# Loads of v tied to a mask of the slot, and one weight load moved behind a later product, in a threshold attention with SwiGLU

## The chip, the core and the metric

One core of a Trainium2 chip runs the whole program. The metric is the device time of one execution in microseconds, the median of several runs. The engines are named as in the profile: PE (TensorE, with PEld for its weight loads), DVE (VectorE), ACT (ScalarE), POOL (GpSimd) and SP (SyncE, which here only issues DMAs). All work of an engine runs in the order in which the program lists it, and an instruction whose semaphores are not yet reached holds up everything behind it on that engine.

## The reference

```python
batch, n_heads, seq, head_dim = (8, 8, 576, 64)
n_tokens, d_model, d_ff = (4608, 512, 1536)

scores = scale * np.matmul(q, k.transpose(0, 1, 3, 2))
thresh = np.max(scores, axis=-1, keepdims=True) - tau
scores = np.where(scores >= thresh, scores, -1000000000.0)
scores = scores - np.max(scores, axis=-1, keepdims=True)
attn = np.exp(scores)
attn = attn / (np.sum(attn, axis=-1, keepdims=True) + 1e-09)
attn_out = np.matmul(attn, v)
x = attn_out.transpose(0, 2, 1, 3).reshape(B * S, H * D)
g = x @ w_gate
silu = g * (1.0 / (1.0 + np.exp(-g)))
out = (silu * (x @ w_val)) @ w_out
```

q, k and v are 32-bit floats; the weights arrive as 64-bit floats.

## The kernel before

The attention of batch b+1 runs beside the feed-forward of batch b. After a first stretch (about 130 us) in which the first batch's attention is begun and the weights are turned into 32-bit numbers, the main loop runs over 28 pairs of heads, `halved`, with three slots each (`x` = 0, 1, 2), so twelve slots (`kk` = 0 to 11) make up a block `b` of one batch. In a slot TensorE computes scores of a third of the queries (`slot_scores`, L1865), VectorE finds the row maxima (L1886, L1888), ScalarE takes exponentials (L1911), VectorE masks them against the threshold and sums them (`masks`, L1913, six to a slot, one for each head and query group), ScalarE or POOL divides by the sums, and VectorE turns the result (L1941).

The product with v of a pair, `attend` (L1946, its matmuls on L1962), is issued in slot `x` = 1 of the next pair, just ahead of that slot's scores. It reads `vall`, which has one place for a pair's v. `prepare_v` therefore loads the v of the current pair after this product, by four DMAs of 144 KB (`load_v`, L441) on SP's queue. That v is read by the `attend` of the following pair.

Between the scores TensorE runs the feed-forward: gates and values in groups (`Group`, products on L1052, seven products `p1`, `p5`, `p2`, `p6`, `p3`, `p7`, `p4` for a group), and output products (`Outputs` on L1331 in the first blocks, `Deep` with its nested products on L1598 in the later ones). From the third batch on (`DEEP`) the weights of a group and sums of them are streamed from memory into `flow`, which has room for two groups. `load_flow` (L982, its DMA on L985) loads a group in two parts: part 0 is 1024 KB (the first four operands), part 1 is 768 KB (the last three, read by the group's `p3`, `p7` and `p4`). Inside `Deep` the same room holds intermediate sums, so `next_flow` (L1838) asks for the next block's groups 0 and 1 as the output products free it.

`Deep.steps` is `p1, gates_end, p2, p7, p6, p4, p5, p3`. `CD` says how many of these steps are done in which slot: the last two, `p5` and `p3`, fall in slots `kk` = 0 and 1 of the next block. Right behind `p3` the gates of the next block begin.

The order of the instructions on VectorE, ScalarE, POOL and SP is made by `Plan`: each piece of work is a `job` with an engine, an assumed duration, the jobs it depends on and a rank, and the planner lists them by the times it computes. TensorE's order is as written. A job's dependencies decide only the order. What an instruction waits for on the chip follows from the data: a DMA into `vall` waits for the matmuls that still read it, and for an earlier write to the same place.

```python
        if x == 1 and n > 0:
            prepare_v(seg, attend(halved[n - 1]))
```

Of the kernel before, what the change touches and what calls it, by code (L numbers as in the profile page):

```python
# [27 lines left out]
class Plan:  # L28
# [12 lines left out]
    def job(self, eng, took, fn, *deps, rank=1, lag=0.0, moves=0.0):  # L41
        j = Job(eng, took, fn, rank, lag, moves)
        for d in deps:
            if isinstance(d, Job) and d.end is None:
                d.then.append(j)
                j.waits += 1
            elif d is not None:
                j.ready = max(j.ready, self.after(d, eng) if isinstance(d, Job) else d + self.HOP)
        if not j.waits:
            self.open[eng].append(j)  # L50
        return j
# [45 lines left out]
    def pe(self, took, fn, *deps):  # L97
        self.force(*deps)
        for d in deps:
            if d is not None:  # L100
                self.t = max(self.t, (d.end if isinstance(d, Job) else d) + self.HOP)
        self.run(self.t)
        fn()
        self.t += took
        return self.t + self.PIPE
# [39 lines left out]
def kernel(  # L145
# [11 lines left out]
    nc = tc.nc  # L157
# [51 lines left out]
    vall = const.tile([P, 2 * NJ * D], F32, name="vall")  # L209
# [627 lines left out]
    job, pe = plan.job, plan.pe  # L837
# [42 lines left out]
    def take(name, full=False):  # L880
        free = [b for b in banks if (not b.held if b.fixed is not None else b.n in turns)]
        if full:
            free = [b for b in free if b.full]
            return Hold(min(free, key=Bank.free_at), name) if free else None
        n = sum(b.full for b in free)
        return Hold(min(free, key=lambda b: (b.full and n == 1, max(b.free_at(), plan.t))), name)
# [17 lines left out]
    def pool_tt(out, a, b, op):  # L904
        return lambda: nc.gpsimd.tensor_tensor(out=out, in0=a, in1=b, op=op)  # L905
# [84 lines left out]
    def x_place(c, kh):  # L990
        lo = c % 2 * XW if kh == 0 else 2 * XW
        return xall[:, lo:lo + XW].rearrange("p (t c n) -> p t c n", t=2, c=2)
# [42 lines left out]
    class Group:  # L1035
# [32 lines left out]
        def p5(self):  # L1068
            self.take_b()
            self.e = take("pe")  # L1070
            m = self.mul(self.e, self.w[2], xs[0], True, *self.w_deps[2], *ready_x[self.c][1], *self.e.deps)
            self.e.bank.full = True
            s, old = turn_of(s_bufs)
            self.s = s
            self.s5 = job("ACT", 0.55, lambda: nc.scalar.activation(s.ap, self.e.rows(), AF.Copy, scale=0.5), m, *old, rank=0)
# [38 lines left out]
        def p3(self):  # L1114
            m = self.mul(self.e, self.w[5], xs[2], False, self.s5, *self.w_deps[5], *ready_x[self.c][4])
            u = self.u1_buf
            g1 = job("DVE", 0.7, lambda: nc.vector.scalar_tensor_tensor(out=u.ap, in0=self.e.rows(), scalar=0.5, in1=u.ap, op0=ALU.mult,
                                                                        op1=ALU.add), m, self.u1, rank=0)
            self.e.read_by(g1)
            self.e.done(True)  # L1120
            self.finish(0, u, g1, self.a, self.m2)
# [405 lines left out]
    class Deep:  # L1527
# [250 lines left out]

        def p5(self):
            m = self.nested(4, self.x, False, *self.c6)  # L1780
            self.next_flow(1, 1, m)
            t, t7 = self.spaces[0:2]
            self.c5 = self.copies(t, self.x, m, *self.z)
            n, j = self.combine(t7, job("POOL", 2.2, pool_tt(t7, t7, t, ALU.add), *self.c5, *self.c7, rank=1))
            self.ship(1, 1, n, j)
            for b in u_list:
                b.jobs = [*b.jobs, j]

        def p3(self):
            m = self.nested(2, self.x, False, *self.c5)  # L1790
            n, j = self.combine(self.x, m, psum=True)
            self.done(self.x, j)
            self.ship(0, 1, n, j)
# [52 lines left out]
    sc_users = []  # L1846
# [99 lines left out]
    def attend(seg):  # L1946
        i = seg["i"]
        b, cc = divmod(i, NP)
        base = seg["p"]
        p = pall[:, base:base + 2 * NK * SH].rearrange("p (k h j q) -> p h k j q", h=2, j=NK, q=G)  # L1950
        vr = seg["v"]
        R, rows = 2, P // 2
        holds = [take("xa") for _ in range(R)]
        assert cc < 2 or "last_product" not in state

        def fn():
            for j in range(NK):
                for a in range(R):
                    rs = slice(a * rows, (a + 1) * rows)
                    for x in range(NG):  # L1960
                        h, ds = x // 2, slice(x % 2 * G, (x % 2 + 1) * G)
                        nc.tensor.matmul(holds[a].ap()[x * G:(x + 1) * G, 0:SH].rearrange("d (i q) -> d i q", q=G),  # L1962
                                         vr[rs, h, j, ds], p[rs, h, :, j, :], start=(j == 0), stop=(j == NK - 1))

        m = pe(4.5, fn, *seg["turned"], seg["vj"], *holds[0].deps, *holds[1].deps)
        kh, c2 = divmod(cc, 2)
        xk = x_place(b, kh)[:, :, c2, :].rearrange("p t (i a q) -> p a t i q", a=2, q=G)
        xl = xlast[:, cc, :].rearrange("p (a q) -> p a q", a=2)
        js = x_jobs.setdefault(b, [])
        lo, at_last = 0, 2 * NT * G  # L1970
        for a in range(R):
            def copy(a=a):
                nc.scalar.copy(xk[:, a], holds[a].ap()[:, lo:lo + 2 * NT * G].rearrange("p (t i q) -> p t i q", t=2, q=G))
                nc.scalar.copy(xl[:, a], holds[a].ap()[:, at_last:at_last + G])
            js.append(job("ACT", 0.65, copy, m, last_store[0] if cc == 0 else None,
                           *(sixth_kept if b == DEEP + 1 else ()), rank=0))
            holds[a].read_by(js[-1])
            holds[a].done(False)
            holds[a].bank.full = False
        if cc == NP - 1:  # L1980
            store_last(b, *js)
        if cc >= 2:
            token_sums(b, c2, js[2 * c2:2 * c2 + 2] + js[2 * cc:] + [stores[2]], "DVE" if tail[0] else "POOL")
        return m

    def store_last(b, *deps):
        w = S - SM
        last_store[0] = job("SP", 0.1, lambda: nc.sync.dma_start(out=last_hbm[:, :, b * w:(b + 1) * w], in_=xlast), *deps, lag=3.0)
# [24 lines left out]
    def prepare_v(seg, *deps):  # L2013
        seg["vj"] = job("SP", 1.7, lambda: load_v(seg), *deps, lag=2.3, moves=2.6)

    halved = segs[2 * NP:]
# [107 lines left out]
    for s, (n, x) in enumerate((n, x) for n in range(len(halved)) for x in range(NU3)):  # L2124
        seg = halved[n]
        i, t = seg["i"], seg["tiles"][x]
        b, kk = s // NS + 1, s % NS
        if x == 1 and n > 0:
            prepare_v(seg, attend(halved[n - 1]))
        pss, mark = slot_scores(seg, t)  # L2130
        if s == 0:
            next(last, None)
            attend_tile()
            next(last, None)
            flip()
            plan.t += 2.4
            plan.free.update(DVE=2.0, ACT=2.5)
        elif s == 1:
            box = []
            m = pe(1.0, lambda: attend_tile(lambda *y: box.extend(y)))  # L2140
            j = job("ACT", 0.27, box[1], m, rank=0)
            banks[taken[id(box[0])][0]].jobs.append(j)
            give_back(box[0])
            next(last, None)
            store_last(0, j)
        if s == 1:
            prepare_v(seg)
        at_, pooled, max_by_act = (kk, POOLED, MAX_BY_ACT) if b > DEEP else (s, FIRST_POOLED, FIRST_MAX_BY_ACT)
        slot_rest(seg, t, pss, mark, pooled.get(at_, 0), at_ in max_by_act, 1 if x == NU3 - 1 else 2)
        if x == 0 and n + 1 < len(halved):  # L2150
            prepare_next(i + 1, plan.t)
        if s == 0:
            joins = rest_of_weights()
        block_part(b, kk)
        if 2 <= s < 6:
            output_sums(s - 2, plan.t, *joins)
        if s in WS:
            g, place = WS[s]
            weight_sums(g, place, plan.t, *joins, stores.get({2: 0, 3: 1, 4: 3, 5: 4}.get(g)))
        if 10 <= s < 10 + NF2:  # L2160
            g = s - 10
            weight_part(g, summed_g[g], plan.t)
        if s > NS and x and (g := (s - NS) * (NU3 - 1) // NU3) < NF2:
            store_plain(g, parts[g], plan.t)
# [71 lines left out]
```

## Time and profile before

| | us |
|---|---|
| median of 3 runs | 1360.17 (1358.74 to 1366.19) |
| profiled execution | 1362.1 |
| its span, first to last instruction | 1360.2 |
| granted TensorE clock, mean | 0.999 |
| an attention product (L1962), 144 records | 4.39 |
| scores of a slot (L1865), 64 records | 1.63 |
| eight records of a gate product (L1052, 128x256) | 1.73 |
| 768 KB weight load `big<-sums_hbm`, issue to landing, median | 4.4 |
| 1024 KB weight load, issue to landing, median | 5.3 |
| 144 KB load of v, issue to landing, median | 2.9 |

A "record" is one line of the trace; each 32-bit matmul of the program leaves two of TensorE's matmuls and two weight loads. The profile has a page with shares by engine, by slice of the span and by chain, and the trace behind it can be asked for the waits of one engine, for instructions in order of time, and for busy time in given stretches. In a timeline each row has the start, the time it took, the engine, the source line, the operation, what was written from what, and a count; a bracket has the engine's idle time ahead of it and what ended it. "Issue" there means that nothing which the profile shows was waited for. For a DMA issue on SP's queue (SPq) the time is that of issuing; the transfer follows.

TensorE's rows overlap by some 0.1 us where one matmul starts before the last one's modelled end.

### The profile page before, as it was taken

The numbers are of one execution on the slowest core, as the hardware profiler recorded it, in microseconds if no ns is written. First come the engines' busy times: TensorE is split into PE (matmuls) and PEld (weight loads), VectorE is DVE, ScalarE is ACT, GpSimd is POOL, SyncE is SP. The second block draws the span as 40 slices with busy tenths as digits, with TensorE's granted clock in tenths as the row PEclk, the third lists the DMA queues.
The fourth block names the chain that finished last, engine by engine and source line by source line (L and its number), as shares of the span: only waits on it lengthen the run. The fifth ranks groups of instructions, "written<-read, shape, count | busy, mean of one in ns | idle before, by whom it ended". The sixth has DMA issues, their size and how long they took to land.

```text
span 1360.2 us, 39655 instructions
## 1 busy us (share of the span) xinstructions
PE 1341.3 (99%) x15770; PEld 1115.8 (82%) x15770; DVE 1072.6 (79%) x2839; ACT 876.0 (64%) x2260; POOL 689.1 (51%) x717
## 2 busy tenths in 40 slices
PE   8999999999999999999999999999999999999998
PEld 6777777787788788878887888878887789999998
DVE  6888898878887777778787877877787776787786
ACT  6888777777756767677776766776767774330330
POOL 2588397543464669624982379426952495000000
PEclk9999999999999999999999999999999999999999
DMA  8752424555525532554164515553255405424411
GB/s 196 183 187 93 81 56 134 149 137 145 152 68 162 148 98 68 152 159 127 37 188 129 150 36 147 137 151 87 89 156 145 114 22 174 158 78 147 157 61 32
DMA packets 210760, 166.28 MB, mean 122 GB/s; under 512 B 166288, under 2 KB 182160, under 8 KB 205200
## 3 DMA queue, kind: packets, MB, share of 16 engines
q1 hardware_dynamic: 206656, 162.83, 42.2%
q8 instruction: 125, 2.05, 0.6%
q10 hardware_dynamic: 3920, 0.92, 0.4%
q14 instruction: 59, 0.48, 0.1%
HBM read 141.30 MB, written 22.41 MB: 120 GB/s over the span
## 4 chain that ended last, share of the span: by engine, by line
PE 94%; DVE 2%; POOL 1%; DMA 1%; issue 1%; ACT 0%; DVEq 0%; SPq 0%; POOLq 0%
PE pb L1052 18%; PE pa L1052 12%; PE px L1598 12%; PE sc L1865 10%; PE xa L1962 9%; PE pe L1052 9%; PE po L1331 5%; PE py L1598 3%; PE pv L1256 2%; PE pg L1256 2%; PE sc L1213 2%; PE py L1607 2%; PE sc L468 1%; PE pe L1213 1%; PE tp L538 1%; PE xa L569 1%
## 5 line engine op out<-in xcount | busy, mean ns | idle before, releaser
L1913 DVE SCALAR_TENSOR_TENSOR pall<-sc,th,pall 128x288 f32<-128x288 f32 x504 | 244.4, 513 | 58.4 <-ACT pall L1911 39.9
L1052 PE MATMUL pb<-xall,big 128*128 128x256 f32 x1152 | 273.3, 380 | 0.0
L1911 ACT ACTIVATE pall<-sc,nm 128x288 f32<-128x288 f32 x504 | 232.8, 497 | 39.0 <-DVE pall L1913 38.9
L1052 PEld LDWEIGHTS pb<-xall,big 128*128 128x128 f32 x1152 | 216.5, 190 | 30.7 <-issue 2.2
L1941 DVE STREAM_TRANSPOSE pall<-pall 128x576 f32<-128x576 f32 x252 | 188.9, 764 | 30.7 <-ACT pall L1939 22.3
L1939 ACT ACTIVATE pall<-pall,ri 128x288 f32<-128x288 f32 x413 | 189.9, 528 | 30.8 <-DVE ri L1927 30.4
L1052 PE MATMUL pa<-xall,big 128*128 128x256 f32 x768 | 183.6, 382 | 0.0
L905 POOL TENSOR_TENSOR hall<-hall,tmp 128x512 f32<-128x512 f32 x80 | 102.5, 1282 | 155.3 <-DVE hall L1105 137.1
L1886 DVE TENSOR_REDUCE mx<-sc 128x2 f32<-128x576 f32 x168 | 125.7, 748 | 52.4 <-PE sc L1865 52.2
L1052 PEld LDWEIGHTS pa<-xall,big 128*128 128x128 f32 x768 | 142.9, 190 | 22.4 <-issue 2.7
L1865 PE MATMUL sc<-kT,qT 64*32 64x288 f32 (+1 forms) x5376 | 147.1, 345 | 5.0 <-issue 3.4
L1865 PEld LDWEIGHTS sc<-kT,qT 64*32 64x32 f32 x5376 | 95.9, 106 | 57.1 <-issue 18.4
L1052 PE MATMUL pe<-xall,big 128*128 128x256 f32 x576 | 137.3, 381 | 0.0
L1962 PE MATMUL xa<-pall,vall 64*32 64x288 f32 x4032 | 129.3, 404 | 0.6 <-issue 0.6
L1052 PEld LDWEIGHTS pe<-xall,big 128*128 128x128 f32 x576 | 108.4, 190 | 17.0 <-issue 2.5
L1962 PEld LDWEIGHTS xa<-pall,vall 64*32 64x32 f32 x4032 | 74.0, 107 | 48.2 <-issue 6.8
L1936 POOL TENSOR_SCALAR pall<-pall,ri 128x288 f32<-128x288 f32 x91 | 45.2, 511 | 93.3 <-DVE ri L1927 92.9
L1921 ACT COPY sums<-sums 32x6 f32<-32x6 f32 x336 | 66.6, 198 | 36.8 <-DVE pall L1913 31.9
L905 POOL TENSOR_TENSOR tmp<-tmp 128x512 f32<-128x512 f32 (+1 forms) x41 | 56.5, 1377 | 63.7 <-ACT tmp L1127 62.2
L905 POOL TENSOR_TENSOR big<-hall 128x384 f32<-128x384 f32 (+2 forms) x69 | 65.3, 970 | 33.2 <-PE pa L1052 26.1
L1104 ACT ACTIVATE vall<-tmp 128x512 f32<-128x512 f32 x96 | 60.1, 629 | 27.8 <-POOL tmp L905 13.5
L1888 DVE TENSOR_REDUCE mx<-sc 128x1 f32<-128x288 f32 x168 | 75.0, 447 | 0.0
(279 smaller groups left out, 2503.2 us busy)
## 6 DMA issues: line engine op xcount, KB each, us to landing
big<-sums_hbm SPq DMA_DIRECT2D x42, 1024.0 KB, 5.3
big<-sums_hbm SPq DMA_DIRECT2D x48, 768.0 KB, 4.4
vall<-in_v_dram SPq DMA_DIRECT2D x112, 144.0 KB, 2.9
out_dram<-big SPq DMA_DIRECT2D x32, 256.0 KB, 2.4
qT<-in_q_dram SPq DMA_DIRECT2D x112, 72.0 KB, 4.8
kT<-in_k_dram SPq DMA_DIRECT2D x112, 72.0 KB, 2.9
wo<-in_moe_w_gate_dram SPq DMA_DIRECT2D x16, 384.0 KB, 3.5
wo<-in_moe_w_val_dram SPq DMA_DIRECT2D x16, 384.0 KB, 4.1
```

Source lines behind the costliest of these rows:

```text
L905: return lambda: nc.gpsimd.tensor_tensor(out=out, in0=a, in1=b, op=op)
L1052: nc.tensor.matmul(ps[:, i], w[:, k_, i * P:(i + 1) * P], x[:, k_, :], start=first and i == k_ == 0, stop=True, skip_group_check=True)
L1331: nc.tensor.matmul(ps, h(f), w[:, f, :], start=(f == 0), stop=(f == NF2 - 1))
L1598: nc.tensor.matmul(ps, a[:, f, :], ws[n][:, f, :], start=bank_ not in begun, stop=True, skip_group_check=True)
L1865: nc.tensor.matmul(pss[h][(slice(g * G, (g + 1) * G), *part)], qT[hs, col:col + G], kT[hs, c * SH + keys[0]:c * SH + keys[1]], start=True, ...
L1886: rs.append(job("DVE", 0.72, lambda n=n, tile_=tile_: nc.vector.tensor_reduce(out=mx[:, n:n + 2, 0], in_=tile_[:, :, 0:SH], axis=AX.X, op= ...
L1888: rs.append(job("DVE", 0.42, lambda n=n, tile_=tile_: nc.vector.tensor_reduce(out=mx[:, n + 2:n + 3, 0], in_=tile_[:, :, SH:SH + SQ], axis ...
L1911: ej = job("ACT", 0.42, lambda x=x, n=n: nc.scalar.activation(ps[x], scs[x], AF.Exp, bias=nm[:, n:n + 1]), ej, masks.get((h, u - 1)), rank=0)
L1913: masks[x] = job("DVE", 0.45, lambda x=x, n=n: nc.vector.scalar_tensor_tensor(out=ps[x], in0=scs[x], scalar=th[:, n:n + 1], in1=ps[x], op0 ...
L1939: scaled.append(job("ACT", 0.46, lambda x=x, n=n: nc.scalar.activation(x, x, AF.Copy, scale=ri[:, n:n + 1]), rj, rank=rank))
L1941: seg["turned"].append(job("DVE", 0.72, lambda both=both: nc.vector.transpose(out=both, in_=both), *scaled, rank=rank))
L1962: nc.tensor.matmul(holds[a].ap()[x * G:(x + 1) * G, 0:SH].rearrange("d (i q) -> d i q", q=G), vr[rs, h, j, ds], p[rs, h, :, j, :], start=( ...
```

## The change

```diff
--- before.py
+++ after.py
@@ -1778,7 +1778,6 @@
 
         def p5(self):
             m = self.nested(4, self.x, False, *self.c6)
-            self.next_flow(1, 1, m)
             t, t7 = self.spaces[0:2]
             self.c5 = self.copies(t, self.x, m, *self.z)
             n, j = self.combine(t7, job("POOL", 2.2, pool_tt(t7, t7, t, ALU.add), *self.c5, *self.c7, rank=1))
@@ -1788,6 +1787,7 @@
 
         def p3(self):
             m = self.nested(2, self.x, False, *self.c5)
+            self.next_flow(1, 1, m)
             n, j = self.combine(self.x, m, psum=True)
             self.done(self.x, j)
             self.ship(0, 1, n, j)
@@ -2126,7 +2126,7 @@
         i, t = seg["i"], seg["tiles"][x]
         b, kk = s // NS + 1, s % NS
         if x == 1 and n > 0:
-            prepare_v(seg, attend(halved[n - 1]))
+            attended = attend(halved[n - 1])
         pss, mark = slot_scores(seg, t)
         if s == 0:
             next(last, None)
@@ -2147,6 +2147,8 @@
             prepare_v(seg)
         at_, pooled, max_by_act = (kk, POOLED, MAX_BY_ACT) if b > DEEP else (s, FIRST_POOLED, FIRST_MAX_BY_ACT)
         slot_rest(seg, t, pss, mark, pooled.get(at_, 0), at_ in max_by_act, 1 if x == NU3 - 1 else 2)
+        if x == 1 and n > 0:
+            prepare_v(seg, job("DVE", 0.07, lambda: nc.vector.memset(vall[:, 0:1], 0.0), attended, sc_users[2], rank=0))
         if x == 0 and n + 1 < len(halved):
             prepare_next(i + 1, plan.t)
         if s == 0:
```

Two things change. The load of part 1 of the next block's group 1 depends on the output product `p3` in place of `p5`, so the planner lists it later on SP's queue; it does so for the five times that these two methods are used. And for pairs 1 to 27 the four DMAs of v depend on a new VectorE job: a memset of the first column of `vall` in all 128 partitions. That memset depends on the attention product and on the third mask of the slot (`sc_users` holds the slot's masks in the order in which they were made). The column it clears lies in the place that all four DMAs write, so on the chip the first of them waits for the memset; the loaded values then overwrite it.

## The prediction

> **What bounds the kernel now.** I read the page's shares first, then the list of TensorE's waits, then the timelines of TensorE and of SyncE's DMA issues around the longest of those waits, and last the trace's single DMA packets.
>
> ```profile
> PE 1341.3 (99%) x15770; PEld 1115.8 (82%) x15770; DVE 1072.6 (79%) x2839; ACT 876.0 (64%) x2260; POOL 689.1 (51%) x717
> ...
> q8 instruction: 125, 2.05, 0.6%
> ...
> PE 94%; DVE 2%; POOL 1%; DMA 1%; issue 1%; ACT 0%; DVEq 0%; SPq 0%; POOLq 0%
> ```
>
> TensorE is busy for 1341.3 of 1360.2 us and the chain that ended last is TensorE for 94%. Laid side by side, the old and the changed program have TensorE's 7929 matmuls and 541 waits in one and the same order. So the change adds and removes no TensorE work; it can only move the 18.9 us (1360.2 - 1341.3) in which TensorE stood, and most of these lie in the first 145 us, which the change does not touch.
>
> ```profile
> PE sc L1865 <- issue: 3.4, 5, 1.5
> ...
> PE sc L1865 <- DVE pall L1913: 1.6, 1, 1.6
> ...
> PE xa L1962 <- issue: 0.6, 1, 0.6
> ```
>
> After the start only the six "issue" gaps are left (the 1.6 us stand at 141 us). "Issue" means that no semaphore was waited for. TensorE's timeline shows where the longest one lies, and that the same place one block later has none:
>
> ```profile
> 555.20 4.59 PE L1962 MATMUL xa<-pall,vall 64*32 64x288 f32 x144
> 559.59 1.65 PE L1865 MATMUL sc<-kT,qT 64*32 64x288 f32 x58
> 562.70 0.44 PE L1865 MATMUL sc<-kT,qT 64*32 64x144 f32 x6 [1.46 <-issue]
> ...
> 702.01 4.60 PE L1962 MATMUL xa<-pall,vall 64*32 64x288 f32 x144
> 706.40 1.70 PE L1865 MATMUL sc<-kT,qT 64*32 64x288 f32 x64
> ```
>
> From start to start, in place of the printed idle time that begins at a modelled end, the six gaps are 0.52 (at 340.5 us), 0.61 (452.1), 1.74 (561.0), 1.03 (743.2), 0.49 (783.3) and 1.42 us (999.6): 5.81 us together. I counted TensorE's records (weight loads, matmuls, waits) up to each: 7617, 10433, 13505, 18369, 19393, 25537. All leave 193 when divided by 256. The queue "instruction" moved 125 packets of 16 KB (2.05 MB / 125), one per 257 of TensorE's 32081 records (2 x 15770 + 541). So the gaps are TensorE waiting for its next 16 KB of program. The packet records agree: before each gap the packet starts only 61 to 115 records ahead of its boundary, against a median of 238 over all, takes 0.9 us, and TensorE goes on 1.25 to 1.6 us after it. The earliest packets start some 290 records ahead; I call that "due". In this kernel's fastest stretch, an attention product (L1962, 288 records in 4.4 us) followed by scores (L1865, 128 in 1.6 us), those 290 records last only 4.2 to 4.6 us, and 0.9 + 1.4 of them are the packet's own; it may start about 2 us late at most. What makes it later is seen on SyncE's queue:
>
> ```profile
> 555.33 0.35 SPq L985 DMA_DIRECT2D big<-sums_hbm  x1
> 556.00 0.41 SPq L1659 DMA_DIRECT2D out_dram<-big  x1
> 559.83 2.68 SPq L441 DMA_DIRECT2D vall<-in_v_dram  x4
> 562.60 0.57 SPq L1988 DMA_DIRECT2D last_hbm<-xlast  x1
> 564.79 6.71 SPq L1659 DMA_DIRECT2D out_dram<-big  x2
> ```
>
> The 768 KB weight load at 555.33 lands at 560.3. The program packet, due at 556.7, starts at 560.3, 3.6 us late. The pattern repeats at the other five: a 768 or 1024 KB load issued at 335.1, 445.4, 735.7, 777.9 and 993.9, and the packet 2.7 to 4.0 us late. In all six the v load (L441) is issued over 3 us after the packet was due (559.83 against 556.7, 998.4 against 995.3). By that reading v is not the cause.
>
> **The change, part by part.** *The weight load.* `next_flow(1, 1)` is the load at 555.33 (768 KB). In the changed program it stands behind the output store that waits for POOL until 564.78, so it is issued at about 565.2, past the scores, while TensorE is in the output product `p3` (L1598, 563.1 to 568.0), where records run slowly. There are five such loads: 555.3, 702.1, 849.0, 993.9 and 1138.6. Removed: the gap at 561.0 (1.74 us) and the one at 999.6 (1.42 us), 3.16 us. The other three sites have no gap to remove: at 706.4 the scores ran x64 without one, since the boundary falls elsewhere against the load. What the packet now finds ahead of it at 556.7 is the 256 KB store of 556.00; such stores land in a median 2.4 us, so the packet starts by 558.4 and its records are there by 560.7, just ahead of 561.0. The bound on this: from all 3.16 us down to 2.6 if each of the two still shows a quarter of a us.
>
> Does the load then come late? It lands 4.9 us after issue (555.33 to 560.3), so at 570.1; its first reader is the second group's `p3`, whose product starts at 590.5. Cover 20 us. In the last block it goes from 1138.6 to about 1145.4 and lands by 1151; VectorE's sums of it (L908 `pall<-big`) stood at 1150.1 and may slip 1 us; TensorE needs them at 1161.2. Cost 0.
>
> *The loads of v.* 27 memsets of 128x1 are new. VectorE's groups have the masks beside which they stand, and one memset of this size:
>
> ```profile
> L1913 DVE SCALAR_TENSOR_TENSOR pall<-sc,th,pall 128x288 f32<-128x288 f32 x504 | 244.4, 513 | 58.4 <-ACT pall L1911 39.9
> ...
> L202 DVE MEMSET minus<- 128x1 f32 x1 | 0.1, 59 | 0.0
> ```
>
> 27 x 0.059 = 1.6 us on an engine with 288 us idle. Each stands between the third and fourth of a slot's masks (L1913), or behind a sum of an output product; behind it on VectorE wait the other masks, and for these the next scores. In blocks 3 to 7 the last mask ends 0.58 us or more before the next scores in the slots that get a memset (608.36 against 608.94 is the least), which covers 0.06. In block 1 and 2 two such slots have no cover (248.24 against 248.25, 279.87 against 279.86): 2 x 0.06 = 0.12 us, the bounds being 0 and 0.3 if a memset costs as much as two of its rows there.
>
> The load itself moves from the product's end to the mask: 559.83 to about 569.0, 598.72 to 606.3, 636.25 to 643.7; 7 to 9 us. Its four DMAs take 1.7 to 2.7 us to issue and 2.9 us to land; the next product that reads v starts 25 us later (594.1), 19 us in the closest pair (1118.9 to 1138.4). Cost 0. Behind v on SyncE: weight loads, which in the changed order stand ahead of v or wait for a later TensorE product anyway (462.2 against v's issue until 461.2; 609.0 against 608.0; 755.3 against 754.2), the loads of q and k, which move by up to 8 us in one place (352.3 to about 356 to 360, first read on POOL at 379.9), and eight 256 KB stores there. Gain: by the reading above, 0. Its other bound: if v's packets delay the program packet's last 1.3 us, the four gaps that keep their weight load shrink too, by 0.52 + 0.61 + 1.03 + 0.49 = 2.65 us at most. I take 0, because at 743 us TensorE stood already 0.45 us before v's first issue (743.68). Loss: v now runs where another program packet may be due. I went through all the boundaries: 23 have a stretch of 290 records that lasts 7.1 us or less, and none of their packets is due less than 16 us after a new v load. Those due within 5 us of one have 10.6 us or more (due 681.6, needed 692.3). Bound: one new gap of the size seen, 1.7 us.
>
> **The sum.** -3.16 + 0.12 = -3.0 us. The profiled execution took 1362.1 us (span 1360.2, 1.9 around it), so 1359.1 in a profile. The runs' median is 1360.17, 1.9 lower; I take the same 3.0 us from it: 1357.1 us, -0.22%. Parts' bounds: -2.6 to -5.8 for the gaps, +1.7 for a new one.
>
> [...]
>
> **Rivals.** *A, v's packets matter as well:* all six gaps go, 1360.2 - 5.8 + 0.1 = 1354.5. For it: v is issued close to each gap. Against: the start of each packet was late before v. *B, nothing moves:* the gaps are hidden or made again a little elsewhere, or unprofiled runs hardly have them, 1360.2 + 0.1 = 1360.3. For it: three of five sites had no gap, so their coming hangs on alignment, and the median lies 1.9 us under the profile's time. Against: program order and alignment do not change. *C, slower: v meets program packets.* The mechanism is the same gap at new places: 3.3 us of v transfer with a weight load next to it (606.3 and 609.0; 752.5 and 755.3) ahead of a due packet. Each costs up to 1.7 us; from two new gaps on the 3.0 are eaten, and four blocks with two each, 8 x 1.7 = 13.6 less 3.0, give 1370.8. Against: these places lie in slow products, where 290 records last 10.6 to 18 us. *D, the edit does not do what it says*, v still going out at the product's end, is excluded by the order: the load waits for the memset's semaphore.
>
> **How the numbers follow.** Forecast 0.70, A 0.12, B 0.12, C 0.06. The three runs before spread over 7.4 us, so I add 1.5 us of measurement to each side of A and B (1354.5, 1360.3): range 1353 to 1361.8, which leaves out most of C and stray runs. 0.5% is 6.8 us, about what a measurement of this kernel tells from no change. Faster by more needs all six gaps and luck: 0.06. Slower by more is C and a disturbed measurement: 0.06. Within: 0.88.
>
> **What would show it.** Right: TensorE's waits list "issue" on L1865 falls from five to three with no 1.5; scores after the products at 555 and 994 take 1.6 us; L985 issues behind the stores at about 565 and 1004; v about 8 us after each attention product; the gaps near 340, 452, 743, 783 stay. Wrong: those go as well (A), new "issue" gaps 0 to 4 us after a v load (C), or waits of TensorE for VectorE or a DMA.

## The result, and the profile after

The changed kernel took a median of 1355.51 us in 8 runs (1354.37 to 1358.71), the kernel before 1361.61 us in 8 runs beside them (1358.04 to 1366.19): ratio 0.9961, 95% interval 0.9947 to 0.9975, or -5.3 us (-7.2 to -3.4). Two more sets of runs of the changed kernel gave 0.9971 (0.9959 to 0.9982) and 0.9963 (0.9949 to 0.9976). The mean of the three is -4.8 us, where -3.0 was forecast.

The page of the changed kernel has these lines for the ones shown before: shares, program packets, the chain.

```profile
PE 1340.1 (99%) x15770; PEld 1115.7 (82%) x15770; DVE 1071.9 (79%) x2866; ACT 874.9 (65%) x2260; POOL 688.3 (51%) x717
...
q8 instruction: 125, 2.05, 0.6%
...
PE 93%; DVE 2%; DMA 1%; POOL 1%; ACT 1%; issue 0%; SPq 0%; ACTq 0%; DVEq 0%; POOLq 0%
```

TensorE has the same 15770 matmuls and weight loads, the program the same 125 packets, and "issue" fell from 1% of the chain to 0%. The 27 more VectorE instructions are the memsets. TensorE's waits (engine, line, what was waited for: us in total, times, longest) show it by line:

```profile
PE sc L1865 <- issue: 0.9, 2, 0.5
PE sc L1865 <- DVE pall L1913: 0.7, 1, 0.7
```

"Issue" on L1865 was 3.4 us in five pieces with a longest of 1.5, and 0.6 us more on L1962, which has no such line now. Three pieces on L1865 were forecast; the third, 0.34 us near 450, is too short for this list. The second line is the wait in the first 145 us, ahead of anything that was changed. The timeline of TensorE around the place where the longest gap was, and that of SyncE's issues there:

```profile
552.49 4.60 PE L1962 MATMUL xa<-pall,vall 64*32 64x288 f32 x144
556.88 1.70 PE L1865 MATMUL sc<-kT,qT 64*32 64x288 f32 x64
```

```profile
553.27 0.41 SPq L1659 DMA_DIRECT2D out_dram<-big  x1
557.98 0.56 SPq L1988 DMA_DIRECT2D last_hbm<-xlast  x1
562.10 0.41 SPq L1659 DMA_DIRECT2D out_dram<-big  x1
562.61 0.42 SPq L985 DMA_DIRECT2D big<-sums_hbm  x1
564.47 1.75 SPq L441 DMA_DIRECT2D vall<-in_v_dram  x4
```

The scores run x64 without a break where they broke after x58. The weight load (L985) stands 5.7 us behind the scores' start in place of 4.3 us ahead of it (555.33 against 559.59), and v (L441) goes out 7.6 us after the scores' start.

Where the 6.6 us between the two spans (1360.2 and 1353.6) come from can be read off TensorE's records, since both programs list the same ones. TensorE reached its 2362nd record, in the first block of the main loop, 2.64 us earlier (150.93 against 153.57), before any part of the change has run. From there to record 32000 it took 1191.64 against 1195.86 us: 4.22 less. Behind that it lost 0.2. The gaps at boundaries of program packets, from start to start, make up nearly all of the 4.22:

| kernel | near 340 | 452 | 561 | 743 | 783 | 1000 us | elsewhere | sum | records 2362 to 32000 | ratio to before |
|---|---|---|---|---|---|---|---|---|---|---|
| before | 0.52 | 0.61 | 1.74 | 1.03 | 0.49 | 1.42 | | 5.81 | 1195.9 | |
| before, again | 0.81 | 0.34 | 2.03 | - | 0.75 | 2.27 | | 6.20 | 1197.6 | |
| changed | 0.70 | 0.34 | - | - | 0.77 | - | | 1.81 | 1191.6 | 0.9961 |
| changed, again | 0.53 | - | - | - | 0.83 | - | | 1.36 | 1190.8 | 0.9971 |
| changed, third | 0.43 | 0.84 | - | - | 0.54 | - | | 1.81 | 1191.4 | 0.9963 |
| load alone | 0.47 | 0.30 | - | - | 0.75 | - | | 1.52 | 1191.3 | 0.9956 |
| load alone, again | 0.82 | 0.83 | - | - | 1.25 | - | | 2.90 | 1193.1 | 0.9976 |
| v alone | 0.71 | - | 1.74 | - | 0.56 | 1.72 | | 4.73 | 1194.8 | 0.9996 |
| 256 KB more | 0.62 | - | 2.03 | - | 1.31 | 1.98 | | 5.94 | 1197.4 | 1.0010 |
| 24 records fewer | 0.57 | - | 0.74 | - | 0.56 | 1.29 | 2.18 at 850 | 5.34 | 1196.1 | 0.9993 |
| 80 records more | - | - | - | - | - | - | 0.82 at 494, 1.74 at 711, 1.00 at 932 | 3.56 | 1193.3 | 1.0030 |
| all loads held | - | - | - | - | 1.42 | - | | 1.42 | 1195.5 | 0.9983 |
| sums and part 1 held | - | - | - | - | - | - | | 0 | 1189.2 | 0.9960 |
| the same, again | - | - | - | - | - | - | | 0 | 1189.3 | 0.9963 |

(One profile for each row; gaps over 0.26 us at these boundaries after 145 us; a dash is none. The kernel before, again, ran once, for its profile. The record counts of the two shifted kernels are taken with their shift. The kernel with all loads held waits for other things as well, told below.) Two of the six gaps were forecast to go, 561 and 1000, and went. A third, 743, went too.

### The profile page after: what moved, and what is told of

Its sections match the earlier page's. It is cut to its first block, busy times and chain, and to the rows that moved or that the text cites. A ratio compares the mean times of both kernels' runs of the same rounds, so it can differ in the third digit from the quotient of the medians.

```text
span 1353.6 us, 39678 instructions
## 1 busy us (share of the span) xinstructions
PE 1340.1 (99%) x15770; PEld 1115.7 (82%) x15770; DVE 1071.9 (79%) x2866; ACT 874.9 (65%) x2260; POOL 688.3 (51%) x717
## 4 chain that ended last, share of the span: by engine, by line
PE 93%; DVE 2%; DMA 1%; POOL 1%; ACT 1%; issue 0%; SPq 0%; ACTq 0%; DVEq 0%; POOLq 0%
PE pb L1052 19%; PE pa L1052 13%; PE px L1598 12%; PE sc L1865 10%; PE xa L1962 9%; PE pe L1052 9%; PE po L1331 6%; PE py L1598 3%; PE pv L1256 2%; PE pg L1256 2%; PE sc L1213 2%; PE py L1607 2%; PE sc L468 1%; PE pe L1213 1%; PE tp L538 1%; PE xa L569 1%
## 5 line engine op out<-in xcount | busy, mean ns | idle before, releaser
L1052 PE MATMUL pb<-xall,big 128*128 128x256 f32 x1152 | 273.3, 380 | 0.0
L1052 PEld LDWEIGHTS pb<-xall,big 128*128 128x128 f32 x1152 | 216.5, 190 | 30.7 <-issue 2.2
L1052 PE MATMUL pa<-xall,big 128*128 128x256 f32 x768 | 183.5, 382 | 0.0
L1052 PEld LDWEIGHTS pa<-xall,big 128*128 128x128 f32 x768 | 142.9, 190 | 22.4 <-issue 2.2
L1865 PE MATMUL sc<-kT,qT 64*32 64x288 f32 (+1 forms) x5376 | 146.1, 345 | 1.6 <-issue 0.9
L1865 PEld LDWEIGHTS sc<-kT,qT 64*32 64x32 f32 x5376 | 95.8, 106 | 53.0 <-issue 15.5
L1052 PE MATMUL pe<-xall,big 128*128 128x256 f32 x576 | 137.3, 381 | 0.0
L1962 PE MATMUL xa<-pall,vall 64*32 64x288 f32 x4032 | 128.9, 404 | 0.0
L1052 PEld LDWEIGHTS pe<-xall,big 128*128 128x128 f32 x576 | 108.5, 190 | 17.0 <-issue 2.5
L1962 PEld LDWEIGHTS xa<-pall,vall 64*32 64x32 f32 x4032 | 74.0, 107 | 47.1 <-issue 5.6
```

Of the source, the lines that this page charges most:

```text
L1052: nc.tensor.matmul(ps[:, i], w[:, k_, i * P:(i + 1) * P], x[:, k_, :], start=first and i == k_ == 0, stop=True, skip_group_check=True)
L1865: nc.tensor.matmul(pss[h][(slice(g * G, (g + 1) * G), *part)], qT[hs, col:col + G], kT[hs, c * SH + keys[0]:c * SH + keys[1]], start=True, ...
```

## The experiments

### Which of the two parts

The load alone: `next_flow(1, 1, m)` moved from `p5` to `p3`, the loads of v left as they were.

```diff
         def p5(self):
             m = self.nested(4, self.x, False, *self.c6)
-            self.next_flow(1, 1, m)
...
         def p3(self):
             m = self.nested(2, self.x, False, *self.c5)
+            self.next_flow(1, 1, m)
```

> Only the load next_flow(1, 1) is moved, from p5 to p3; the loads of v stay as they were before. Theory (TensorE waits for a 16 KB program packet that stands behind a weight load issued before the packet was due): the gaps at 561.0 and 999.6 go, the other four stay near 340, 452, 743 and 783 us, time -2.6 to -3.2 us against before (ratio about 0.9977). If the gap at 743 goes here too, it is not v that removed it in the changed kernel. Rival (the packets of v delay the program): four to six gaps stay, time 0 to -1 us, and the measured -5 us must come from v.

Measured: ratio 0.9956 (0.9943 to 0.9968). The gaps at 561, 743 and 1000 are gone, the three others stand. Two of these were forecast to go. That 743 went too, and that the gain is about twice the expected -2.6 to -3.2 us, was not forecast. A second set of runs:

> The kernel with the load alone moved, once more, beside the next variant. Theory: gaps near 337, 449 and 777 us again, 1.3 to 2.0 us together, none at 555, 739 and 991; ratio to before 0.995 to 0.997, so that its gain is the whole gain of the change.

Measured: 0.9976 (0.9967 to 0.9985), less gain than expected, the same three sites with 2.90 us, more than the 2.0 expected. The two sets average -4.6 us and the changed kernel's three -4.8, so the load alone carries the gain.

V alone:

```diff
-            prepare_v(seg, attend(halved[n - 1]))
+            attended = attend(halved[n - 1])
...
+        if x == 1 and n > 0:
+            prepare_v(seg, job("DVE", 0.07, lambda: nc.vector.memset(vall[:, 0:1], 0.0), attended, sc_users[2], rank=0))
```

> Only the loads of v wait for the memset; next_flow(1, 1) stays in p5. Theory (a weight load ahead of the program packet): all six gaps stay where they were, 561.0 with 1.7 and 999.6 with 1.4 us, time 0 to +0.2 us (ratio 0.9999 to 1.0002). Rival (v's packets delay the program): the gaps go or shrink to under half, time -2.5 to -5.8 us (ratio 0.998 to 0.9957). If only the gap at 743 goes, v is the cause of that one: -1.0 us.

Measured: 0.9996 (0.9987 to 1.0005), -0.5 us (-1.8 to +0.7). TensorE's timeline in this kernel, and SyncE's:

```profile
557.36 1.65 PE L1865 MATMUL sc<-kT,qT 64*32 64x288 f32 x58
560.47 0.44 PE L1865 MATMUL sc<-kT,qT 64*32 64x144 f32 x6 [1.45 <-issue]
```

```profile
553.11 0.35 SPq L985 DMA_DIRECT2D big<-sums_hbm  x1
553.76 0.41 SPq L1659 DMA_DIRECT2D out_dram<-big  x1
...
566.78 1.76 SPq L441 DMA_DIRECT2D vall<-in_v_dram  x4
```

V is issued 6.3 us after the gap, and the gap has its old 1.74 us (558.73 to 560.47): v has no part in it. But 743 has no gap here either, as with the load alone, so that neither part of the change explains it; the kernel before, run again, does.

### The same kernels again

> The kernel before once more, to tell what of a single profile repeats. Theory: the gaps at 340, 452, 561, 783 and 1000 us stand again within 0.3 us, since transfer and packet meet there by the order of the program. Open: whether the gap at 743 us (1.03 us) and the slower first 23 us (TensorE's 200th record at 22.1 us, 20.5 in the changed kernel) come again; if both do, 1.0 and 1.6 us of the measured gain belong to the two kernels and not to chance; if not, they are chance.

Neither came again: no gap at 743, and TensorE's 200th record at 20.49 us, as in the changed kernel. In the first profile the 1024 KB load that was issued at 735.72 had a long tail: the 16 DMA engines were busy to 51, 23, 11 and 5% in the half microseconds from 740 us on, and the program packet began at 741.9. That site has 6.6 us from the packet's request (what the prediction calls due, here taken 302 records ahead of the boundary, as explained below) to need, 1.9 more than at 340. The load was issued 0.9 us ahead of the request, and its last packet ended 5.3 us after the request. In the nine other profiles that issue it 0.8 to 0.9 us ahead, one of them with the kernel's old order throughout (256 KB more), it ended after 3.9 to 4.5 us, the program packet began after 3.2 to 4.5, and no gap over 0.26 us followed. In the repeat the load was issued 0.2 us behind the request, and the packet began after 1.9 us. So 1.0 and 1.6 of the 6.6 us between the first two profiles are chance. Against this the two gaps in question were larger here, 2.03 and 2.27; the second is 0.85 us larger than in the first profile, where 0.3 was expected.

> The changed kernel once more, in more runs and beside the variants. Theory: gaps near 338, 450 and 778 us again (0.3 to 0.8 us each), none at 555, 739 and 991; ratio to before 0.995 to 0.997, and the same as with the load alone moved within 1.2 us.

Measured: 0.9971, at the edge of what was expected, gaps at 339 and 778 us, none at 450 this time.

### Shifting the program against the work

If the gaps are waits for program packets, they must move when each 16 KB boundary falls at another place in the work, with every later instruction unchanged. The kernel before begins with six idle matmuls that only occupy TensorE. In one kernel they are left out, in the other there are 26, 23 of them on 16 columns:

```diff
-    run_idle(6)
+    run_idle(0)
```

```diff
-        for _ in range(n):
-            nc.tensor.matmul(ps[:, 0:TC], ones[:, 0:P], ones, start=True, stop=True)
+        for w in [TC] * n if n == 6 else [TC] * 3 + [16] * 23 if n else []:
+            nc.tensor.matmul(ps[:, 0:w], ones[:, 0:P], ones[:, 0:w], start=True, stop=True)
...
-    run_idle(6)
+    run_idle(26)
```

> The kernel before, without the six idle matmuls at its start (24 TensorE records, in a time in which TensorE waits anyway); every later instruction on every engine is the same, only each 16 KB boundary of TensorE's program falls 24 records later in the work. Theory: worked out from the trace of before for this shift (a packet starts at its due time 290 records ahead, or when the load issued ahead of it has landed, and TensorE can go on 1.6 us later), none of the boundaries falls late any more: all six gaps go, 0 to 0.3 us left of 5.8, time -5 to -6 us (ratio 0.996). Rival (the gaps are contention or a wait tied to these places, whatever the program's layout): the gaps stay at 340, 452, 561, 743, 783 and 1000 us and the time is the same within 0.5 us.

> The kernel before with 26 idle matmuls in place of six at its start (three as before, 23 of 16 columns): 80 TensorE records more, so each 16 KB boundary falls 80 records earlier in the work. Theory: worked out from the trace of before for this shift, gaps of 0.5 to 2.1 us near 452, 490, 561, 709, 891, 929 and 999 us, none near 340 and 783 us, 9.6 us together by the same reckoning that gives 4.7 for the layout before (measured 5.8); time +4 to +5 us (ratio 1.003 to 1.004). Rival (gaps tied to places, not to the program's layout): gaps as before, time 0 to +0.5 us.

Measured: 0.9993 (0.9985 to 1.0002) and 1.0030 (1.0018 to 1.0043). The places moved, in both. With 80 records more, none of the six old sites has a gap, and the third site of `next_flow(1, 1)`, which ran x64 without one before, has one:

```profile
704.88 4.59 PE L1962 MATMUL xa<-pall,vall 64*32 64x288 f32 x144
709.26 1.67 PE L1865 MATMUL sc<-kT,qT 64*32 64x288 f32 x61
712.39 0.43 PE L1865 MATMUL sc<-kT,qT 64*32 64x144 f32 x3 [1.45 <-issue]
```

The load (L985) had been issued 4.25 us ahead of those scores, and the break comes after x61:

```profile
705.01 0.42 SPq L985 DMA_DIRECT2D big<-sums_hbm  x1
705.66 0.41 SPq L1659 DMA_DIRECT2D out_dram<-big  x1
```

With 24 records fewer, two breaks moved out of the scores into the output product behind them (L1598), 24 records later in the work, and a new one of 2.18 us opened at 850. In both kernels, counted by their own records, all the gaps leave 193 when divided by 256. A wait tied to a place or to contention does not do that; this rival is out.

The forecast sizes failed. For 24 fewer 0 to 0.3 us were expected and 5.3 stand; for 80 more three of seven sites came. The reckoning took each boundary's time from the trace of before with its stalls in it, so that work just behind an old gap seemed to have 1.4 to 1.7 us to spare, and it took the request 290 records ahead. Laid over six traces, the undisturbed packets scatter least when the request is put 302 records ahead; they then start 0.5 us or more after it. With that and the stalls taken out, the same reckoning finds four of the five sites of 24 fewer, all but the one at 850, and the three of 80 more, but also sites that have no gap (those near 452 and 886 among them), and some of its sizes are off by half a microsecond and more. It was fitted afterwards and not tried on a new shift.

The site at 850, which is one of the five of `next_flow(1, 1)`, shows how close such a meeting is. With 24 records fewer, TensorE and SyncE:

```profile
848.73 1.17 PE L1865 MATMUL sc<-kT,qT 64*32 64x288 f32 x28
851.68 1.17 PE L1865 MATMUL sc<-kT,qT 64*32 64x288 f32 x36 [1.78 <-issue]
```

```profile
844.51 0.56 SPq L985 DMA_DIRECT2D big<-sums_hbm  x1
```

The load is issued 0.36 us ahead of the packet's request, and the packet began 4.39 us after that request. In the four profiles that have the load in `p5` and the old layout it is issued 0.08 us behind the request, and the packet began after 1.15 to 1.52 us.

The times of the two kernels as a whole test little: the 26 products took 12.55 us on TensorE in place of 4.56, so its work began some 7 us later than before, and without the six the start was slow as well (200th record of before at 23.1 us). That the ratio of 80 more lies in the expected range is therefore luck. The stretch behind is what counts: 1193.3 us with 80 more, 2.6 less than before, where its sum of gaps is 2.25 less.

### More in front of the packet

A transfer of 256 KB more behind each of the five loads, memory to memory:

```diff
+            out=flow[:, s + lo * HW:s + to * HW], in_=sums_hbm[g][:, lo * HW:to * HW])] + [nc.sync.dma_start(out=more_hbm, in_=sums_hbm[g][:, 0:HW]) for _ in range(two)], ...
...
-            self.next_flow(1, 1, m)
+            dosed[0] = True; self.next_flow(1, 1, m); dosed[0] = False
```

> The kernel before, with one more transfer of 256 KB (memory to memory, read by nobody) right behind each of the five loads next_flow(1, 1) in p5. Theory (the packet starts 0.65 us before the transfer ahead of it has landed, whatever is computed meanwhile): the packets at 561 and 1000 us start 1 to 1.5 us later than the 560.3 and 998.8 of before, so these two gaps grow from 1.7 and 1.4 to 2.7 to 3.2 us; no new gap at the three other sites, whose packets have 2 us and more to spare; time +2 to +3 us (ratio 1.0015 to 1.0022), if the gap at 743 stays. Rival (the wait there is TensorE's own, or v's): these two gaps stay within 0.3 us of their size.

Measured: 1.0010 (0.9999 to 1.0022), gaps of 2.03 and 1.98 us. That is inside what the two sites show without the transfer (1.42 to 2.27), so the expected growth did not come, and the added transfer had no effect that can be told. The packets began 4.05 and 3.89 us after their requests, against 3.49 to 4.16 in the kernels without it, about when the 768 KB load landed (0.2 and 0.0 us after) and 0.5 to 0.7 us before the added transfer did. It had been issued 0.75 to 0.95 us ahead of the request. The store of 256 KB (L1659) in the changed kernel, issued 0.7 us ahead, costs its packets little if anything: they begin 1.25 to 1.44 us after the request, where the undisturbed ones have a median of 1.1. So "waits for what is queued ahead of it" is too wide. What the traces have at every gap of the table is a load of 768 or 1024 KB issued 0.36 to 2.1 us ahead of the request, and a packet that begins between 1.0 us ahead of that load's landing and 0.4 us behind it. At other boundaries, which had time enough, a packet began up to 3.9 us ahead of the landing, so it does not always wait for the load's end. By what rule the two share the way, and why a smaller transfer behind the load costs nothing, is left open.

### Taking the other gaps away

Two tries. In the first, all loads of weights and sums asked for in the slot ahead of an attention product were kept back and listed behind the next v:

```diff
+            if hold_on[0]:
+                held.append(lambda *more: fn(*args, *more))
...
+            while held:
+                held.pop(0)(sc_users[3])
+        hold_on[0] = x == 0 and n > 0
```

> The changed kernel, and in every slot that comes ahead of an attention product the loads of weights and sums (load_flow, load_sums) are kept back and listed behind the next load of v, so that none is queued when the program packet of the attention product is requested. Theory: the three gaps that are left near 338, 450 and 778 us (1.8 us together) go too, no gap over 0.3 us after 145 us; -1.5 to -2 us against the changed kernel (ratio to before 0.9945 to 0.995). Against it: a load that now comes 8 to 12 us later may be late for its group, or meet another packet; then a wait on a DMA at L1052, or a gap at another place, shows, and the time is the changed kernel's or worse.

Measured: 0.9983 (0.9971 to 0.9995), where the changed kernel beside it had 0.9971, and from record 2362 to 32000 it took 4 us more: worse than the changed kernel. The gaps at 338 and 450 went, that at 782 grew to 1.42, because there the planner listed the load ahead of v and nothing on the chip held it. And the other side of the expectation came. TensorE's waits have two new lines (L1064 is L1052 of the other kernels):

```profile
PE pa L1064 <- DMA big<-sums_hbm: 2.3, 4, 0.7
PE pe L1064 <- DMA big<-sums_hbm: 0.5, 1, 0.5
```

The gates wait 2.8 us for weight loads that now come late: a load that was asked for just in time cannot be held.

The second try starts from the load alone moved, holds sums and part 1 only, and makes the hold real on the chip by a memset of the load's own first column:

```diff
+                if hold_on[0] and args[2] != 0:
+                    held.append((fn, args, place(*args)))
...
+        for fn, args, to in held:
+            fn(*args, job("DVE", 0.07, lambda to=to: nc.vector.memset(to, 0.0), sc_users[0], ..., rank=0))
+        held.clear()
+        hold_on[0] = x == 0 and n > 0
```

> The kernel with the load alone moved (next_flow(1, 1) in p3, loads of v as before), and besides it the loads that are asked for ahead of an attention product, sums and part 1 only, wait for a memset of the first column of their place, which depends on the first mask of the slot: they go out some 3 us behind the scores in place of just ahead of the product. The 1024 KB loads (part 0) stay, since keeping them back made the gates wait for a DMA. Theory: the gaps near 337 and 777 us (0.5 and 0.75 us) go, the one near 449 (a 1024 KB load stands ahead of it) stays at 0.3 to 0.6; -1.2 us against the kernel with the load alone moved (TensorE's 2362nd to its 32000th record: 1191.3 there, 1190.0 to 1190.3 here), ratio to before 0.9947 to 0.996. Against it: a wait on a DMA at L1052, or a new gap elsewhere.

Measured: 0.9960 (0.9947 to 0.9973), median 1354.90 us, and no gap at any boundary. The site at 778, TensorE and SyncE (L1879 is L1865, L1066 is L1052, L999 is L985):

```profile
770.99 4.60 PE L1976 MATMUL xa<-pall,vall 64*32 64x288 f32 x144
775.38 1.70 PE L1879 MATMUL sc<-kT,qT 64*32 64x288 f32 x64
777.01 1.99 PE L1066 MATMUL pe<-xall,big 128*128 128x256 f32 x8
```

```profile
775.62 1.73 SPq L441 DMA_DIRECT2D vall<-in_v_dram  x4
781.94 0.34 SPq L999 DMA_DIRECT2D big<-sums_hbm  x1
```

The load is issued 5 us behind the scores, v is issued during them, and the scores run x64 unbroken. The gap near 449 was expected to stay and did not: the 1024 KB load still stands ahead of that packet, issued 2.06 and 2.45 us before the request where it was 1.1 to 2.1 in the profiles that have the gap, and the packet came just in time. That site is on the edge and is not settled by this.

> The kernel without gaps once more, beside the changed kernel on one chip. Theory: no gap over 0.3 us between 145 us and the end again (TensorE's 2362nd to 32000th record 1189.2 to 1189.6 us), ratio to before 0.995 to 0.997, and 1.4 to 1.8 us less than the changed kernel. Against it: the gaps were absent by chance; then one to three of 0.3 to 1 us stand near 338, 449 and 778 us and the two kernels take the same.

> The changed kernel a third time, on the chip of the kernel without gaps. Theory: gaps near 338, 450 and 778 us, 1.4 to 2.9 us together, and the stretch from TensorE's 2362nd to its 32000th record that much longer than in the other kernel; ratio to before 0.996 to 0.9975.

Measured beside each other: 0.9963 (0.9951 to 0.9976), median 1354.91, and 0.9963 (0.9949 to 0.9976), median 1355.36. From record 2362 to 32000 the kernel without gaps took 1189.24 and 1189.30 us, the changed one 1191.64, 1190.84 and 1191.41: 2.0 us less on average, and the same in both of its profiles within 0.06. In the whole runs the 0.5 to 1 us between the medians is less than either interval: its profiles are the shortest, but that it beats the changed kernel in whole runs is not shown.

## Why the prediction was right, and what was mis-sized

**The bound and the mechanism held.** TensorE's order did not change, and behind the start the time moved by its packet waits and, in one profile, by its clock. With the gaps taken out, stretches of 1000 records from 2362 on agree between the kernels before, changed, load alone and v alone within 0.02 us in most and within 0.25 us in all but two: 0.43 us behind 740 in the second profile of the load alone, and 1.74 us, told below.

**The two gaps.** Forecast to go: those at 561.0 and 999.6, because the load leaves their packets' way. They went in all eight profiles with the load moved, and stand in all that keep it in `p5` at the old layout of the program. With 80 records more they are gone too, with the load in `p5`: it takes both, the load and the boundary. The 256 KB store did less than feared: the lower bound of 2.6 us wasn't needed, and neither site shows a rest.

**The mis-sized term** is these 3.16 us. They were read from one profile, in which both gaps were small: 1.74 and 1.42. The other two profiles with this order have 2.03 and 2.27, and 1.74 and 1.72. And behind a gap of some 2 us there can be a second price, the clock, that the sum did not have: 1.74 us in the repeat of before. So the same two sites cost 3.2, 6.0 and 3.5 us, 4.2 on average, and the gap at 743 adds its 1.0 in one profile of three. That comes to 4.6 us, against 4.8 measured; three profiles make this a rough agreement. The prediction's other bound on the gaps, -5.8 for all six, was left for rival A, but the place to widen was this term.

**743** was to stay, because its load does not move. It was no rule but a chance (above). The prediction counted 743 with the sites that have 4.2 to 4.6 us from due to need, but in its own trace that site has 5.35 us (737.88 to 743.23), so an ordinary delay does not reach TensorE there (the packets that began 3.2 to 4.5 us after their request left no gap over 0.26 us). The reading of v from it, that TensorE stood before v's first issue, was sound, and the alone runs confirm it.

**The loads of v: 0, right.** Rival A would have had the four other gaps go; three stand, and v alone leaves the two large ones as they were. The 27 memsets took 59 ns each, as reckoned, and the 0.12 us for two of them without cover do not show: in the first two blocks the 1000-record stretches of changed and before agree to 0.01 us. New gaps behind v loads (rival C) are in no profile. The load's own reader, 20 us later, never waits: no wait on a DMA at L1598 or L1052 is in the changed kernel's list.

**Rival B** had nothing move, the gaps hidden or made again a little elsewhere. Neither was seen: the changed kernel's gaps are 4.00 us less in sum (5.81 to 1.81), its stretch from record 2362 to 32000 took 4.22 less, and no new site has a gap over 0.26 us in its three profiles. In the shifted kernels gaps of 0.56 to 2.18 us move with the 256-record boundaries, so TensorE's waits for its program are not hidden here. Rival B's ground, that the runs' median lies 1.9 us under the profile's time and so hardly has the gaps, is about the size of the first profile's slow start, 1.6 us, which the repeat did not have.

## What to carry to other kernels

When a saturated TensorE stops for "issue", count its records to each stop: if the remainders by 256 agree, as all gaps here left 193, ask whether it waits for its program, and the thing to try is to move the large load (here 768 or 1024 KB) issued just ahead of the packet's request (here 0.36 to 2.1 us ahead, the request some 300 records before the boundary), above all ahead of stretches of small, fast matmuls (at five of the six gaps of before, 290 records in 4.2 to 4.7 us). To keep such a load back, let data hold it on the chip, since a planner's order alone is not a wait: the gap at 782, where nothing held the load, grew to 1.42 us, and with the memset of the second try it was gone. Hold only loads with slack to their first reader: the one that was moved has 20 us, and among those kept back in the first try some had too little, and TensorE waited 2.8 us for them. Take the size of such gaps from several profiles: one shows the place, not the price (1.42, 2.27 and 1.72 us at one boundary).

## What the hardware showed that was not expected

Behind some waits of TensorE of about 2 us, 2.02 to 2.27, its granted clock stood at 0.50 for some 3.4 us. In the repeat of before the gap of 2.27 us ends at 998.6; these are stretches of 1 us behind it (busy time and instructions of PE, PEld, DVE, ACT and POOL, then the granted clock, DMA share and GB/s):

```profile
998.00:999.00 1.00, 0.43 (x6) 0.21 (x5) 0.00 (x0) 0.69 (x2) 1.00 (x3) 0.97 0.77 212
999.00:1000.00 1.00, 1.00 (x6) 1.00 (x6) 0.96 (x2) 0.00 (x0) 0.92 (x2) 0.50 0.87 225
1000.00:1001.00 1.00, 1.00 (x6) 1.00 (x6) 1.00 (x3) 0.00 (x0) 0.10 (x1) 0.50 0.04 8
1001.00:1002.00 1.00, 1.00 (x7) 1.00 (x6) 0.89 (x7) 0.00 (x0) 0.00 (x0) 0.50 0.79 261
```

The granted clock is 0.50 from 999 to 1002 and back at 1.00 from 1002.4. The output product's first twelve records take 2.93 us where they took 1.60 in the first profile:

```profile
998.93 2.93 PE L1598 MATMUL px<-wo,hall 128*128 128x128 f32 x12
```

```profile
1001.35 1.60 PE L1598 MATMUL px<-wo,hall 128*128 128x128 f32 x12
```

The loss is the 1.74 us above. The gap of 2.03 us with 256 KB more lost 1.75 in the same way, with a clock of 0.50 from 561.7 to 565; after the gap of 2.18 us at 850 with 24 records fewer the mean clock is 0.69 from 852 to 855 and 0.61 to 857; the gap of 2.03 at 561 in the repeat of before had no such effect, nor had the one of 1.98 with 256 KB more. At the very start it is the same: before and changed, from 8.4 to 11.7 us, in that order:

```profile
8.40:11.70 3.30, 3.30 (x13) 2.11 (x10) 1.42 (x2) 0.94 (x3) 0.48 (x1) 0.51 0.98 307
```

```profile
8.40:11.70 3.30, 3.30 (x18) 2.40 (x14) 2.28 (x5) 1.74 (x4) 0.48 (x1) 1.00 0.92 298
```

TensorE had waited 2.02 us before it in the one and 1.01 in the other; that is the 1.6 us of the slow start. Of the waits named here those of 2.02, 2.03, 2.18 and 2.27 us were followed by a slow stretch, and two of 2.03 and 1.98 us were not, so the length of the wait alone doesn't decide. What else does is not shown.
